# Attention and soft MoE on one core: one batch-end store, 2.5 groups by halves, smaller last slab pieces, and 32 weight rows on the hardware queue

## The chip, the core and the metric

The kernel runs on one core of one Trainium2 chip. The metric is the device time of one execution in microseconds (us). The kernel before took 181.37 us as the median of six runs (180.99 to 181.56).

The core has five instruction streams: PE (matmul; PEld is its weight load), DVE (vector), ACT (scalar), POOL and SP. The profile counts 16 DMA engines. Two DMA queues matter. The loads of q, k, v and of nearly all weights go from POOL to the software queue, which the profile calls q0, and are cast from f32 to bf16 on the way: in the kernel before the profile has 30.41 MB on q0 for 60.82 MB of f32 (the 61.93 MB read in all, less the 1.11 MB of loads on q1). All stores, the first half of one weight and phi go from SP to the hardware queue, q1. A transfer is cut into packets (18900 in all in the kernel before). A transfer of 128 partitions lands in 16 parts, whose times the trace gives. It does not name the DMA engine of a packet or of a part: where an engine is said to be ahead or late, one of the 16 parts was, and that a part is an engine's is my reading.

## The reference, cut to what matters

```python
# q, k, v: (8 batches, 8 heads, 576 tokens, 64)
scores = q @ k.transpose(0, 1, 3, 2) / 8
# heads 0-3: a causal window of 32; heads 4-7: 128 wide, each fourth key
attn = softmax(where(mask, scores, -1e9)) @ v
x = attn.transpose(0, 2, 1, 3).reshape(4608, 512)        # 4608 = 8 * 576

# soft MoE: 8 experts with 4 slots each; phi (512, 32), w1 (8, 512, 1024), w2 (8, 1024, 512)
logits = x @ phi
slot_input = softmax_over_tokens(logits).T @ x           # (32, 512)
slot_out[e] = relu(slot_input[e] @ w1[e]) @ w2[e]        # four rows for each expert
return softmax_over_slots(logits) @ slot_out             # (4608, 512), f32
```

Two facts shape the end. No output row can be finished before the last part of w2 is there, because each row mixes all slots. And 576 tokens are 4 × 128 + 64, so the last 64 tokens of each batch do not fill 128 partitions with four rows each; the kernel gathers the ends of all eight batches in a ninth group of 512 rows, called the batch-end group here.

## The kernel before

The loads are issued in a fixed order: q, k, v of all batches with w1 between them, then w2. The last expert's w2 comes in two column slabs of 256, each in pieces of 4, 2 and 2 of its eight row chunks.

```python
def w1_piece(e, hf, r0=0, n=2):                 # one half of an expert's w1, all 128 partitions
    def fn():
        return pool.dma_start(
            a(o_w1 + e * 4096 + hf * 2048 + 1024 * r0, [[1, 1024 * n]]),
            moe_w1[e, 256 * hf:256 * hf + 256, :].rearrange("(p two) f -> p (two f)", two=2)
            [:, 1024 * r0:1024 * (r0 + n)])
    return (fn, n << 19, f"w1_{e}{hf}", [b_w1[e]])
# ... cut ...
for s in range(2):
    wq += [w2_slab(6, s), w2_slab(7, s, 0, 4), w2_slab(7, s, 4, 2),
           w2_slab(7, s, 6, 2)]
```

L2 is the product with w2. A tile of output needs its columns of L2's sum. Phase 1 works on columns 0 to 255 and phase 2 on columns 256 to 511; for the first two groups (`NA`) the tiles are made by column halves, so that their first halves can be stored before the last slab has landed.

```python
for x in (1, 2):                                # the two column slabs of experts 6 and 7
    l2((6,), x, 256 * x - 256, 256, bufs=[b_w2[6][x - 1]])
    for y, cs in enumerate((range(4), range(4, 6), range(6, 8))):
        l2((7,), x, 256 * x - 256, 256, cs, [b_w2h[y][x - 1]])
    op(DVE, lambda x=x: dve.tensor_tensor(...))  # adds the earlier experts' sum: "the add"

NA = 2
# ... cut ...
def tok(G, j):                                  # 128 tokens: each fourth of a group of 512
    return (a(o_et + 576 * G + j, [[4, 128]]) if G < 8 else
            a(o_tail + j, [[4, 128]]))

def store(G, c0, cw, prio, j0=0, n=4):
    # ...
    for p0 in [0] if G < 8 else range(0, 128, 16):   # batch ends: eight stores of 16 partitions
        pn = 128 if G < 8 else 16
        dst = out[576 * G:576 * G + 512] if G < 8 else out[36 * p0 + 512:36 * p0 + 576]
        dst = dst[:, c0:c0 + cw].rearrange("(p j) f -> p j f", j=4)
        store_ops.append(op(SP, lambda p0=p0, pn=pn, dst=dst: spq.dma_start(
            dst[:, j0:j0 + n, :],
            af(ostg(G) + 2 * (512 * j0 + c0), [[512, n], [1, cw]], p0, pn)), ...))

halves = [(n // 2, n % 2 * 2) for n in range(int(2 * NA))]
# phase 1: tiles and stores of columns 0-255 of `halves`; phase 2: columns 256-511 of them,
# then whole rows of the other groups in order 2, 3, ..., 8 (the batch ends last)
```

The softmax here doesn't subtract the row's maximum and nothing guards it: scores larger than these inputs give would overflow.

## Time and profile before

| | before |
|---|---|
| time, median of six runs | 181.37 us |
| span of the profiled run, and its granted TensorE clock | 179.8 us, 0.945 |
| last part of w2 ("the last slab") landed | 152.60 us |
| first store that needs it landed | 156.91 us |
| the last full 1 MB store landed | 174.38 us |
| the last batch-end store landed | 179.31 us |

The granted clock is the share of its full speed that PE was allowed; it changes between 0.5 and 1.0 within a run (kernel before: 1.00 to 146.4 us, 0.50 to 153.2, 1.00 to 166.8, then 0.50). The kernel is bound by DMA. These are lines of the page of the kernel before: in the first two, each of the 40 columns is a fortieth of the span; then the queues with packets, MB and share of the time of 16 engines.

```profile
DMA  5999999999999999999999999999999999799995
GB/s 184 233 210 211 214 209 213 215 208 213 213 210 215 212 209 210 215 211 208 215 211 211 215 210 214 214 214 211 215 211 213 197 196 235 243 401 408 425 346 162
...
q0 software_dynamic: 15024, 30.41, 89.6%
q1 hardware_dynamic: 3856, 10.55, 16.5%
...
HBM read 61.93 MB, written 9.44 MB: 397 GB/s over the span
```

Slices 2 to 34 are all 9, full. Then comes a 7 (the change from loads to stores), then stores at 400 GB/s and over, and at the very end 346 and 162 GB/s. (A cast load is counted by its bf16 result, 30.41 MB on q0 for 60.82 MB read, so 213 GB/s there is about 426 GB/s of reading.) PE is busy 70% of the span and DVE 65%, so they wait for DMA. Time can only come from uneven engines, from gaps and from poor transfers. The windows show where these are; the columns are the start and end, the length, each engine's busy time with its instructions, the granted clock, the mean DMA share and the rate.

```profile
core 0: us, PE busy (x) PEld busy (x) DVE busy (x) ACT busy (x) POOL busy (x), PEclk, DMA share, GB/s
...
20.00:24.00 4.00, 3.40 (x77) 2.40 (x76) 3.97 (x8) 3.15 (x4) 1.97 (x4) 1.00 1.08 213
152.60:156.90 4.30, 3.75 (x21) 1.92 (x21) 3.10 (x7) 2.79 (x7) 0.00 (x0) 0.93 0.71 240
155.10:155.60 0.50, 0.50 (x4) 0.30 (x4) 0.50 (x2) 0.50 (x3) 0.00 (x0) 1.00 0.00 0
169.40:171.90 2.50, 0.00 (x0) 0.00 (x0) 0.00 (x0) 0.00 (x0) 0.00 (x0) 0.50 1.01 419
174.40:179.30 4.90, 0.00 (x0) 0.00 (x0) 0.00 (x0) 0.00 (x0) 0.00 (x0) 0.50 0.72 187
```

- **The end.** A 1 MB store of 128 partitions takes 2.50 us at 419 GB/s. The batch ends are 1 MB too, but take 4.9 us at 187 GB/s. No engine works then, so all of it is span. In the trace, 8 KB packets of these eight stores take up to 1.47 us where those of the other stores take 0.31.
- **The gap.** From 155.1 to 155.6 us nothing moves at all. The stores of the first halves have been sent, and those that need the last slab are not ready.
- **The run-up.** The trace gives for each transfer the times at which its 16 parts landed. Around 10 us a load's parts land within 0.5 us; the last slab's lie 2.72 us apart, and fall in two clumps: seven within 0.65 us of the first, one at 1.29, eight at 2.39 to 2.72. The latest part decides when L2 can go on: the last part of the first column slab landed at 147.24 us and the next matmul began at 147.28. Over the run, 16 instruction fetches of 16 KB go out, one each 7 us or so, and each takes 0.9 to 1.0 us. The landings of the kernel before follow them step by step. Before the first fetch (22.52 us) the latest part of a load on q0 is 0.50 to 0.65 us behind the first part; after it one part is 1.62 to 1.79 behind; with each fetch up to the eighth (72.91) there is one more, and then eight are 1.25 to 1.60 behind. After the ninth (80.22) one of them is over 2.6 behind, and after the sixteenth (137.25) eight are, by 2.37 to 2.77. So a fetch puts one part about 1 us back, and the lag of the last slab fits two fetches for each of eight parts. Which engines these are, the trace does not tell.

What the last slab releases is seen in the chain of waits of the kernel before (start, length, what ran) and then in the timeline of DVE (start, length, operation, in brackets the idle time before it and what ended that).

```profile
115.41 31.83 DMA ar<-in_moe_w_dram
147.28 0.62 PE ps L857 x2
147.93 0.44 DVE ar L881
...
150.37 2.89 PE ps L857 x16
153.29 0.44 DVE ar L881
153.77 0.42 PE ps L901 x2
154.22 8.90 DVE ar L913 x15
```

```profile
153.29 0.43 DVE L881 TENSOR_TENSOR ar<-ps,ar 64x256 bf16<-64x256 f32 x1 [2.40 <-PE ps L857]
154.22 4.95 DVE L913 TENSOR_SCALAR ar<-ps,fs 128x256 f32<-128x256 f32 x9 [0.51 <-PE ps L901]
```

The add (line 881) of the last slab starts at 153.29, 0.69 us after the landing at 152.60, behind L2's matmuls (line 857); the first output tiles follow at 154.22. The way from the landing to the first store that needs it (156.91) is 4.31 us.

### The profile page before, as it was taken

The numbers are of one execution on the slowest core, as the hardware profiler recorded it, in microseconds if no ns is written. First come the engines' busy times: TensorE is split into PE (matmuls) and PEld (weight loads), VectorE is DVE, ScalarE is ACT, GpSimd is POOL, SyncE is SP. The second block draws the span as 40 slices with busy tenths as digits, with TensorE's granted clock in tenths as the row PEclk, the third lists the DMA queues.
The fourth block names the chain that finished last, engine by engine and source line by source line (L and its number), as shares of the span: only waits on it lengthen the run. The fifth ranks groups of instructions, "written<-read, shape, count | busy, mean of one in ns | idle before, by whom it ended". The sixth has DMA issues, their size and how long they took to land.

```text
span 179.8 us, 4781 instructions
## 1 busy us (share of the span) xinstructions
PE 125.4 (70%) x2092; PEld 84.5 (47%) x2092; DVE 116.9 (65%) x219; ACT 104.9 (58%) x164; POOL 50.9 (28%) x101
## 2 busy tenths in 40 slices
PE   0008877987989899899789889885775469892000
PEld 0005645764767667666567667674431125420000
DVE  6898789779798798898699699291200104797000
ACT  2406598796798788787688788945020103794000
POOL 7559742242334134133930000951000000000000
PEclk9999999999999999999999999999999975999555
DMA  5999999999999999999999999999999999799995
GB/s 184 233 210 211 214 209 213 215 208 213 213 210 215 212 209 210 215 211 208 215 211 211 215 210 214 214 214 211 215 211 213 197 196 235 243 401 408 425 346 162
DMA packets 18900, 41.26 MB, mean 230 GB/s; under 512 B 1984, under 2 KB 8128, under 8 KB 17984
## 3 DMA queue, kind: packets, MB, share of 16 engines
q0 software_dynamic: 15024, 30.41, 89.6%
q1 hardware_dynamic: 3856, 10.55, 16.5%
q8 instruction: 16, 0.26, 0.5%
q14 instruction: 4, 0.03, 0.0%
HBM read 61.93 MB, written 9.44 MB: 397 GB/s over the span
## 4 chain that ended last, share of the span: by engine, by line
DMA 59%; DVE 20%; PE 6%; ACT 3%; issue 2%; POOL 2%; DVEq 0%
DMA ar<-in_k_dram 41%; DMA ar<-in_moe_w_dram 18%; DVE ar L488 6%; DVE ar L913 6%; DVE ar L614 2%; PE ps L857 2%; DVE ar L445 2%; PE ps L901 1%; POOL ar L371 1%; ACT ar L548 1%; DVE ar L450 1%; PE ps L509 1%; ACT ar L576 1%; ACT ar L670 1%; POOL ar L364 1%
## 5 line engine op out<-in xcount | busy, mean ns | idle before, releaser
L488 DVE STREAM_TRANSPOSE ar<-ar 128x576 uint32<-128x576 uint32 x40 | 48.5, 1239 | 7.7 <-DMA ar<-in_k_dram 7.7
L548 ACT ACTIVATE ar<-ps 128x1152 bf16<-128x1152 f32 (+1 forms) x32 | 38.0, 1186 | 20.6 <-PE ps L533 11.4
L509 PE MATMUL ps<-ar 128*128 128x320 bf16 (+1 forms) x128 | 22.7, 301 | 15.6 <-DVE ar L488 13.1
L614 DVE TENSOR_TENSOR ar<-ps,fs 96x768 bf16<-96x768 f32 (+1 forms) x32 | 26.3, 823 | 1.3
L576 ACT ACTIVATE ar<-ps 128x768 bf16<-128x768 bf16 x32 | 24.8, 810 | 2.2 <-PE ps L570 2.1
L509 PEld LDWEIGHTS ps<-ar 128*128 128x128 bf16 x128 | 10.5, 99 | 20.2 <-POOL ar L418 13.1
L570 PE MATMUL ps<-ar 128*128 128x128 bf16 x192 | 15.9, 229 | 3.8 <-DVE ar L614 3.4
L603 PE MATMUL ps<-ar 128*128 128x65 bf16 x320 | 14.7, 193 | 3.3 <-ACT ar L548 3.2
L910 ACT ACTIVATE ar<-ps,fs 128x512 f32<-128x512 f32 (+1 forms) x22 | 11.4, 656 | 8.7 <-PE ps L901 8.7
L857 PE MATMUL ps<-ar 128*32 128x512 bf16 (+1 forms) x80 | 11.7, 374 | 6.0 <-DMA ar<-in_moe_w_dram 5.4
L335 POOL DMA_DIRECT2D ar<-in_k_dram x16 | 8.9, 555 | 24.8 <-DVE ar L488 15.6
L570 PEld LDWEIGHTS ps<-ar 128*128 128x128 bf16 x192 | 12.4, 118 | 5.7 <-DVE ar L614 4.0
L603 PEld LDWEIGHTS ps<-ar 128*128 128x128 bf16 x320 | 12.0, 97 | 6.0 <-ACT ar L548 3.7
L913 DVE TENSOR_SCALAR ar<-ps,fs 128x512 f32<-128x512 f32 (+1 forms) x22 | 12.6, 649 | 1.3 <-PE ps L901 1.3
L364 POOL DMA_DIRECT2D ar<-in_moe_w_dram x12 | 6.4, 580 | 20.8 <-DVE ar L488 20.8
L335 POOL DMA_DIRECT2D ar<-in_q_dram x16 | 8.8, 547 | 10.5 <-DVE fs L610 5.0
L901 PE MATMUL ps<-ar 128*128 128x512 bf16 (+1 forms) x44 | 10.7, 372 | 1.4 <-DVE ar L881 1.1
L610 DVE RECIPROCAL fs<-ps 96x12 f32<-96x12 f32 (+1 forms) x32 | 6.2, 195 | 7.9 <-PE ps L603 7.6
L670 ACT ACTIVATE ar<-ps 128x576 bf16<-128x576 bf16 x16 | 9.6, 652 | 3.1 <-PE ps L654 3.1
L335 POOL DMA_DIRECT2D ar<-in_v_dram x16 | 8.8, 549 | 8.8 <-DVE fs L610 5.5
L857 PEld LDWEIGHTS ps<-ar 128*32 128x32 bf16 x80 | 5.0, 104 | 12.3 <-DMA ar<-in_moe_w_dram 8.8
L693 PE MATMUL ps<-ar 128*128 128x288 bf16 x64 | 9.2, 287 | 1.2 <-ACT ar L677 1.2
(75 smaller groups left out, 186.7 us busy)
## 6 DMA issues: line engine op xcount, KB each, us to landing
ar<-in_moe_w_dram POOLq DMA_DIRECT2D x29, 512.0 KB, 27.5
out_dram<-ar SPq DMA_DIRECT2D x5, 1024.0 KB, 8.1
ar<-in_k_dram POOLq DMA_DIRECT2D x16, 288.0 KB, 23.4
ar<-in_q_dram POOLq DMA_DIRECT2D x16, 288.0 KB, 23.5
ar<-in_v_dram POOLq DMA_DIRECT2D x16, 288.0 KB, 23.6
out_dram<-ar SPq DMA_DIRECT2D x8, 256.0 KB, 3.4
ar<-in_moe_w_dram SPq DMA_DIRECT2D x1, 1024.0 KB, 5.0
out_dram<-ar SPq DMA_DIRECT2D x2, 512.0 KB, 4.0
```

Source lines behind the costliest of these rows:

```text
L335: return pool.dma_start(a(o_stg + (s * 3 + j) * 1152, [[1, 1152]]), src[b, 4 * dl:4 * dl + 4].rearrange("h (p t) d -> (h p) (t d)", p=32))
L488: return dve.transpose(au(o_dst, [[1, 18], [18, 32]]), au(src, [[32, 18], [1, 32]]))
L509: pe.matmul(pf(h, 0, [[1, W]]), a(o_id, [[1, 128]]), a(msk, [[1, W]]), start=True, stop=False)
L548: eo = op(ACT, lambda P=P, W=W: act.activation(a(P, [[W, 4], [1, W]]), AP(ps, 0, [[4096, 128], [512, 4], [1, W]]), ACTF.Exp, scale=SCALE), ...
L570: last = pe.transpose(pb(bank.idx, bb * 256 + par * 32, [[64, 4], [1, 32]]), src, a(o_id, [[1, 128]]))
L576: op(ACT, lambda t=t, bank=bank: act.activation(a(o_vb[vs] + 3 * t * VBK, [[66, 12], [2, 32], [1, 2]]), pb(bank.idx, 0, [[64, 12], [1, 32] ...
L603: last = pe.matmul(pf(bank.idx + x, 65 * t, [[1, 65]]), w, a(VB + t * VBK + 66 * h, [[1, 65]]), start=True, stop=True)
L614: op(DVE, lambda hp=hp, bank=bank: dve.tensor_tensor(a(ox + 128 * hp, [[64, 2], [256, NT], [1, 64]], 0, rows), pf(bank.idx, 0, [[512, 2], ...
L857: last = pe.matmul(pf(sobank[x].idx, 0, [[1, n]], 32 * j, 32), a(o_htz + 1024 * g + 128 * c + 32 * j, [[1, 32]]), a(w2off(e) + DM * c + co ...
L901: op(PE, lambda: pe.matmul(pf(bank.idx, 0, [[1, cw]]), tok(G, j), a(o_so + c0, [[1, cw]]), start=True, stop=True), pet(1, cw), prio, reads ...
L910: op(ACT, lambda: act.activation(dst, src(), ACTF.Copy, scale=sca), actt(cw, .1), prio + .1, reads=[bank, b_rinv], writes=wr, name=f"OE{G} ...
L913: op(DVE, lambda: dve.tensor_scalar(dst, src(), sca, None, op0=AluOp.mult), dvet(cw, True) + .08, prio + .1, reads=[bank, b_rinv], writes= ...
```

## The change

Its intent: less work after the last slab, a fuller gap, a faster end, and less on the load queue. It has four parts.

1. **One store for the batch ends.** The copy that gathers them puts them in the order (token quad, batch) and the store covers all 128 partitions; its destination has an outer dimension of 16, then 8. It is also moved from the last place to the middle, after group 2.
2. **2.5 groups by halves** for 2: one more 256 KB store (a phase-1 store) ahead of the last slab.
3. **Last slab pieces of 4, 2, 1, 1** for 4, 2, 2.
4. **32 partitions of one w1 piece** (96 to 127 of expert 0's second half) go over the hardware queue as f32, in transfers of five adjacent partitions, to a buffer that is still free; POOL casts them later.

```diff
-    def w1_piece(e, hf, r0=0, n=2):
+    def w1_piece(e, hf):
+        pn = 96 if (e, hf) == (0, 1) else 128
# ... the rest of the piece: [:pn] of the source, partitions 0..pn ...
-               w2_slab(7, s, 6, 2)]
+               w2_slab(7, s, 6, 1), w2_slab(7, s, 7, 1)]
# ... cut ...
+    def load_w1g(after):
+        src = moe_w1[0, 256:512, :].rearrange("(p two) f -> p (two f)", two=2)
+        for p0, pn in [(96 + 5 * n, 5) for n in range(6)] + [(126, 2)]:
+            op(SP, lambda p0=p0, pn=pn: spq.dma_start(
+                af(w2off(3), [[1, 2048]], p0, pn), src[p0:p0 + pn]), ..., writes=b_w2[3], ...)
+        op(POOL, lambda: pool.tensor_copy(
+            a(o_w1 + 2048, [[1, 2048]], 96, 32), af(w2off(3), [[1, 2048]], 96, 32)), ...)
# ... cut: load_w1g(first_t[3]) is called in batch 1 ...
-        a(o_tail, [[64, 8], [1, 64]]), a(o_et + 512, [[576, 8], [1, 64]])), ...
+        a(o_tail, [[4, 8], [32, 16], [1, 4]]), a(o_et + 512, [[576, 8], [4, 16], [1, 4]])), ...
-        for y, cs in enumerate((range(4), range(4, 6), range(6, 8))):
+        for y, cs in enumerate((range(4), range(4, 6), range(6, 7), range(7, 8))):
-    NA = 2
+    NA = 2.5
-        for p0 in [0] if G < 8 else range(0, 128, 16):
# ... cut: the store before, shown above ...
+        if G < 8:
+            dst = out[576 * G:576 * G + 512, c0:c0 + cw].rearrange("(p j) f -> p j f", j=4)[:, j0:j0 + n, :]
+            src = af(ostg(G) + 2 * (512 * j0 + c0), [[512, n], [1, cw]])
+        else:
+            dst = out.rearrange("(b r) f -> b r f", b=8)[:, 512:576, :].rearrange("b (i j) f -> i b (j f)", j=4)
+            src = af(ostg(G), [[1, 2048]])
+        store_ops.append(op(SP, lambda: spq.dma_start(dst, src), ...))
-    for n in range(int(2 * NA), 18):
-        G, x = n // 2, n % 2 * 2
+    for G, x in [(2, 2)] + [(G, x) for G in (8, 3, 4, 5, 6, 7) for x in (0, 2)]:
```

More of the change, by code (lines that the diff above doesn't have):

```diff
@@ L309, in bass_dilated_sliding_attn__then__soft_moe_slots_kernel @@
     b_w5h = [Buf(f"w5h{x}") for x in range(2)]
-    b_w2h = [[Buf(f"w2h{x}{s}") for s in range(2)] for x in range(3)]
+    b_w2h = [[Buf(f"w2h{x}{s}") for s in range(2)] for x in range(4)]
     b_htz, b_tail, b_so = Buf("htz"), Buf("tail"), [Buf("soA"), Buf("soB")]
@@ L351, in w_sem @@
         return shared[key]
-    def w1_piece(e, hf, r0=0, n=2):
+    def w1_piece(e, hf):
+        pn = 96 if (e, hf) == (0, 1) else 128
         def fn():
             return pool.dma_start(
-                a(o_w1 + e * 4096 + hf * 2048 + 1024 * r0, [[1, 1024 * n]]),
-                moe_w1[e, 256 * hf:256 * hf + 256, :].rearrange("(p two) f -> p (two f)", two=2)
-                [:, 1024 * r0:1024 * (r0 + n)])
-        return (fn, n << 19, f"w1_{e}{hf}", [b_w1[e]])
+                a(o_w1 + e * 4096 + hf * 2048, [[1, 2048]], 0, pn),
+                moe_w1[e, 256 * hf:256 * hf + 256, :].rearrange("(p two) f -> p (two f)", two=2)[:pn])
+        return (fn, pn << 13, f"w1_{e}{hf}", [b_w1[e]])
     def w2_piece(e, c0):
@@ L373, in fn @@
                 moe_w2[e].rearrange("(p c) f -> p c f", c=8)[:, c0:c0 + n, 256 * s:256 * s + 256])
-        return (fn, n << 17, f"w2s_{e}{s}{c0}", [b_w2[e][s] if n == 8 else b_w2h[(0, 4, 6).index(c0)][s]])
+        return (fn, n << 17, f"w2s_{e}{s}{c0}", [b_w2[e][s] if n == 8 else b_w2h[(0, 4, 6, 7).index(c0)][s]])
     for e in range(8):
@@ L406, in bass_dilated_sliding_attn__then__soft_moe_slots_kernel @@
             1.1, -200.0, reads=b_w2[4], writes=[b_w1[0]], name=f"w1c{x}")
+    s_w1g = sem("s_w1g")
+    def load_w1g(after):
+        src = moe_w1[0, 256:512, :].rearrange("(p two) f -> p (two f)", two=2)
+        for p0, pn in [(96 + 5 * n, 5) for n in range(6)] + [(126, 2)]:
+            op(SP, lambda p0=p0, pn=pn: spq.dma_start(
+                af(w2off(3), [[1, 2048]], p0, pn), src[p0:p0 + pn]), .1, -50.0, kind="dma",
+               nbytes=pn << 13, lag=4.0, sem=s_w1g, after=[after], writes=b_w2[3], name=f"w1g{p0}")
+        op(POOL, lambda: pool.tensor_copy(
+            a(o_w1 + 2048, [[1, 2048]], 96, 32), af(w2off(3), [[1, 2048]], 96, 32)), 2.5, 0.0,
+           reads=b_w2[3], writes=[b_w1[0]], name="w1gc")
     def const_ops():
@@ L762, in bass_dilated_sliding_attn__then__soft_moe_slots_kernel @@
             load_phi(first_t[0])
+        if i == 1:
+            load_w1g(first_t[3])
     names = [w[2] for w in wq]
@@ L795, in bass_dilated_sliding_attn__then__soft_moe_slots_kernel @@
     op(POOL, lambda: pool.tensor_copy(
-        a(o_tail, [[64, 8], [1, 64]]), a(o_et + 512, [[576, 8], [1, 64]])), .8, T1 + 4, reads=[b_et],
+        a(o_tail, [[4, 8], [32, 16], [1, 4]]), a(o_et + 512, [[576, 8], [4, 16], [1, 4]])), .8, T1 + 4, reads=[b_et],
        writes=[b_tail], name="tail")
@@ L919, in store @@
               if c0 < 256 * (s + 1) and c0 + cw > 256 * s]
-        for p0 in [0] if G < 8 else range(0, 128, 16):
-            pn = 128 if G < 8 else 16
-            dst = out[576 * G:576 * G + 512] if G < 8 else out[36 * p0 + 512:36 * p0 + 576]
-            dst = dst[:, c0:c0 + cw].rearrange("(p j) f -> p j f", j=4)
-            store_ops.append(op(SP, lambda p0=p0, pn=pn, dst=dst: spq.dma_start(
-                dst[:, j0:j0 + n, :],
-                af(ostg(G) + 2 * (512 * j0 + c0), [[512, n], [1, cw]], p0, pn)), .1, prio, kind="dma",
-                nbytes=pn * n * cw * 4, rate=347e3 if cw < 512 else 420e3,
-                sem=sem(f"s_o{G}{c0}{j0}{p0}"), reads=rd, name=f"ST{G}{c0}{j0}{p0}"))
+        if G < 8:
[4 more added lines that the diff above has]
+            src = af(ostg(G), [[1, 2048]])
+        store_ops.append(op(SP, lambda: spq.dma_start(dst, src), .1, prio, kind="dma",
+                            nbytes=128 * n * cw * 4, rate=347e3 if cw < 512 else 420e3,
+                            sem=sem(f"s_o{G}{c0}{j0}"), reads=rd, name=f"ST{G}{c0}{j0}"))
     T2 = T1 + 40
@@ L939, in bass_dilated_sliding_attn__then__soft_moe_slots_kernel @@
         store(G, 256, 256, T2 + 10 + G + .25 * x + .2, x, 2)
-    for n in range(int(2 * NA), 18):
-        G, x = n // 2, n % 2 * 2
+    for G, x in [(2, 2)] + [(G, x) for G in (8, 3, 4, 5, 6, 7) for x in (0, 2)]:
+        at = G if G < 8 else 2.6
         for j in (x, x + 1):
-            out_tile(G, j, 0, 512, T2 + 10 + G + .25 * x)
-        if G == NA:
-            store(G, 0, 512, T2 + 10 + G + .25 * x + .2, x, 2)
+            out_tile(G, j, 0, 512, T2 + 10 + at + .1 * x)
+        if G < NA:
+            store(G, 0, 512, T2 + 10 + at + .1 * x + .1, x, 2)
         elif x:
-            store(G, 0, 512, T2 + 10 + G + .5)
+            store(G, 0, 512, T2 + 10 + at + .3)
     order = sc.run([4, 5, 6, 7], [0, 1, 2, 3], last_ex[0])
```

## The prediction

> **What bounds it now.** DMA. In the page's row of DMA slices every slice from 2 to 34 reads 9; 61.93 MB read and 9.44 MB written make 397 GB/s over the 179.8 us span. PE (70%) and DVE (65%) wait. Time can only come from unevenness, gaps and poor transfers.
>
> Read from the landings of each transfer's 16 parts:
> - The load queue's engines drift apart. A load's first and last part land 0.5 us apart at 10 us, 2.72 us apart at 152.6 us (last slab): then eight engines are 2.4 to 2.7 us behind the first, seven less than 0.7. The sixteen 16 KB instruction fetches, one each 7 us, fit that: about 1.1 us on one engine each.
> - After the last slab (152.60) come L2 matmuls, add and first tiles; the first full store lands at 156.91. First-half stores fill only to 155.39; from 155.1 to 155.6 the DMA share is 0.
> - The eight 128 KB batch-end stores take 174.38 to 179.31, 4.93 us for 1 MB; 1 MB stores of 128 partitions land each 2.50 us. Their 8 KB packets take up to 1.47 us instead of 0.31. [...]
>
> **What the change does.**
> 1. One batch-end store for eight: up to -2.43 us, all on the path. Doubt: the destination's outer dimension is now 16[...], and it could still cost 4.9 us. 65% for the good case.
> 2. 2.5 groups by halves: one more 256 KB store (0.67 to 0.77 us) in the gap, -0.5 us; but two more tiles (0.43 us on ACT and DVE) ahead of the second half's L2, where PE at half clock has 0.1 us of slack: gives back 0.2 to 0.3.
> 3. Pieces 4/2/1/1: one matmul less after the last landing, -0.2 us. POOL's extra issues run 30 us ahead.
> 4. 32 w1 partitions on the hardware queue: 2 rows (0.31 us each) less on all engines, 6 or 7 extra on five. [...] If those are among the engines ahead, the last slab lands 0.6 us earlier; if not, up to 1.3 us later. [...] 70% for the gain. The POOL copy (0.60 us for 512 columns; 2.4 for 2048) is off the path: issues are 23 us ahead of landings.
>
> Attention has slack: L2 waits for w2 from 135.6 us.
>
> **Sum.** All good: -2.4 -0.6 -0.4 = -3.4, 178.0 us. Weighted with the doubts: **178.6 us**, range 177.3 to 180.6. Faster by over 2%: 0.22; within 2%: 0.75; slower by over 2%: 0.03.
>
> **What would show it.** (1) The batch-end store lands 2.5, not 4 to 5, us after the one before; about 419 GB/s to the end. (2) DMA share near 155 us no longer 0; five half stores. (3) One matmul between the last slab's landing and the add. (4) The last slab's parts land within about 2.1 us, the last near 152.0.
>
> **What would make it wrong.** [...]the wrong five engines; PE becoming the limit before the second half; engines that stay uneven through the stores.

Its sum: −2.4 (point 1: 4.93 − 2.50 us), −0.6 (point 4: two rows of 0.31 us less on each engine) and −0.4 (points 2 and 3, net) make −3.4, so 178.0 us from 181.4, and 178.6 with the doubts. That one store could still cost 4.9 us, and that five engines get 6 or 7 rows each, stand as estimates. So do the 2.4 us for the POOL copy, four times its 0.60; it took 1.89 in the kernel after.

## The result, and the profile after

Ratios here are the mean time of one kernel's fast runs over the mean of the other's fast runs of the same rounds, so they are not quite the ratio of the medians that are quoted. Where the text gives a kernel's distance from before in us, it is (ratio − 1) × 181.4.

| | before | after |
|---|---|---|
| time, median of six runs (range) | 181.37 (180.99 to 181.56) | 182.74 (182.17 to 183.23) |
| ratio, 95% interval | | 1.0077 (1.0053 to 1.0102), +1.4 us |
| span of the profiled run, clock | 179.8, 0.945 | 181.2, 0.943 |
| parts of the v load near 30 us: first, last | 27.16, 28.81 | 27.77, 31.79 |
| last slab landed (parts apart) | 152.60 (2.72) | 154.82 (4.26) |
| first store that needs it landed | 156.91 | 158.97 |
| the batch-end store, from the landing before it | 4.93 (eight, last) | 5.04 (one, in the middle) |
| last store landed (parts apart) | 179.31 (1.03) | 180.78 (1.54) |

The kernel after is 0.8% slower. That is inside the "within 2%" class, but outside the predicted range of 177.3 to 180.6.

The last stores of the two profiled runs differ by 1.47 us, and the landings split it. The last slab is 2.22 us later; from it to the first store that needs it the kernel after takes 4.15 us instead of 4.31, so 0.16 less; from there to the end 21.81 instead of 22.40, so 0.59 less. 2.22 − 0.16 − 0.59 = 1.47. All of the loss is there before the last slab lands, and most of it by 32 us.

The page of the kernel after, the same lines as before:

```profile
DMA  5999999999999999999999999999999999899996
GB/s 190 232 208 195 205 180 214 212 210 213 213 211 214 211 210 213 213 210 213 212 210 211 216 208 215 213 215 212 213 214 214 197 195 211 291 363 255 416 427 262
...
q0 software_dynamic: 15024, 30.28, 89.3%
q1 hardware_dynamic: 4208, 10.81, 17.0%
...
HBM read 61.93 MB, written 9.44 MB: 394 GB/s over the span
```

The DMA row looks the same: the row says how long packets are under way, not what they move. The GB/s row shows it. Slices 4 to 6 (about 13.6 to 27 us) read 195, 205, 180 where before has 211, 214, 209. These are the slices in which the w1 rows go over the hardware queue. And the slow stretch of the end, 346 and 162 in the two last slices before, is now the 255 in slice 37, with 262 in the last. The windows of the kernel after:

```profile
core 0: us, PE busy (x) PEld busy (x) DVE busy (x) ACT busy (x) POOL busy (x), PEclk, DMA share, GB/s
...
20.00:24.00 4.00, 3.62 (x78) 2.42 (x76) 3.96 (x7) 2.93 (x4) 1.97 (x4) 1.00 1.18 179
154.80:159.00 4.20, 3.42 (x19) 2.04 (x21) 3.31 (x8) 3.00 (x8) 0.00 (x0) 1.00 0.83 287
157.00:157.50 0.50, 0.35 (x2) 0.30 (x4) 0.50 (x2) 0.50 (x3) 0.00 (x0) 1.00 0.22 76
163.50:168.50 5.00, 1.02 (x3) 0.25 (x3) 3.23 (x5) 1.95 (x4) 0.00 (x0) 0.89 0.97 279
168.50:171.00 2.50, 0.00 (x0) 0.00 (x0) 0.00 (x0) 0.00 (x0) 0.00 (x0) 0.50 1.00 419
178.30:180.80 2.50, 0.00 (x0) 0.00 (x0) 0.00 (x0) 0.00 (x0) 0.00 (x0) 0.50 0.49 206
```

- From 20 to 24 us the DMA share **rose** from 1.08 to 1.18 while the rate **fell** from 213 to 179 GB/s. More packet time is spent on fewer bytes. In the trace the 8 KB packets of the 32 rows take 0.31 to 0.99 us, half of them over 0.71; such a packet by itself takes 0.32.
- The gap near 157 us is partly filled: 76 GB/s and a share of 0.22 where the corresponding stretch before had 0. The whole stretch of 4.2 to 4.3 us after the slab has a share of 0.83 for 0.71.
- From 163.5 to 168.5 us, in which the batch-end store lands and the next one begins, the queue moves 279 GB/s with a share of 0.97. That is again a busy queue that moves little; the stores around it have 419. It no longer stands at the end, but it costs the same, and the last window shows the end ragged.

And the chain of waits and DVE's timeline after, to be read against those of before:

```profile
121.58 33.23 DMA ar<-in_moe_w_dram
154.86 0.30 PE ps L874
155.18 0.44 DVE ar L898
155.67 0.42 PE ps L918 x2
156.12 8.64 DVE ar L930 x15
```

```profile
155.18 0.43 DVE L898 TENSOR_TENSOR ar<-ps,ar 64x256 bf16<-64x256 f32 x1 [2.16 <-PE ps L874]
156.12 5.35 DVE L930 TENSOR_SCALAR ar<-ps,fs 128x256 f32<-128x256 f32 x10 [0.51 <-PE ps L918]
```

One matmul (line 874) of 0.30 us now stands between the landing (154.82) and the add (155.18): 0.36 us for 0.69. Only a third of this is the pieces' doing. The clock granted just after the landing was 0.50 in the kernel before and 1.00 here; d_one_store and e_flat (below), with the old pieces and a clock of 1.00, need 0.47 us, and c_w1g_only, with the old pieces and 0.50, needs 0.63. So the smaller piece is worth 0.11 us and the clock of that run 0.22. The 4.15 us for 4.31 to the first store have the same flaw: d_one_store, with the old pieces, has 4.15 too.

### The profile page after: what moved, and what is told of

It reads as the page before. It is cut to its first block, busy times and chain, and to the rows that moved or that the text cites. A ratio compares the mean times of both kernels' runs of the same rounds, so it can differ in the third digit from the quotient of the medians.

```text
span 181.2 us, 4788 instructions
## 1 busy us (share of the span) xinstructions
PE 126.8 (70%) x2093; PEld 84.9 (47%) x2094; DVE 117.6 (65%) x220; ACT 105.1 (58%) x165; POOL 53.6 (30%) x104
## 4 chain that ended last, share of the span: by engine, by line
DMA 60%; DVE 19%; PE 4%; POOL 4%; issue 2%; ACT 1%; DVEq 0%
DMA ar<-in_k_dram 42%; DMA ar<-in_moe_w_dram 18%; DVE ar L503 6%; DVE ar L930 5%; POOL ar L372 3%; DVE ar L629 2%; DVE ar L460 2%; PE ps L524 2%; DVE ar L465 1%; PE ps L585 1%; PE ps L531 1%; ACT ar L685 1%; ACT ar L563 1%; POOL ar L365 1%; DVE ar L509 1%
## 5 line engine op out<-in xcount | busy, mean ns | idle before, releaser
L503 DVE STREAM_TRANSPOSE ar<-ar 128x576 uint32<-128x576 uint32 x40 | 49.2, 1244 | 10.6 <-DMA ar<-in_k_dram 9.8
L918 PE MATMUL ps<-ar 128*128 128x512 bf16 (+1 forms) x45 | 9.7, 339 | 1.5 <-DVE ar L898 1.0
```

The source lines that it names most:

```text
L503: return dve.transpose(au(o_dst, [[1, 18], [18, 32]]), au(src, [[32, 18], [1, 32]]))
```

## The experiments

All kernels below gave a correct result. Landings are those of each kernel's profiled run. The kernels ran in five groups, and those of one group ran on the same chip beside the kernel before, whose median was 181.54, 181.44, 181.41, 181.30 and 181.36 us in the first to the fifth. Each kernel had 4 to 6 timed runs.

**The theory**: in the transfers of five adjacent partitions the rows slow one another down (the text calls it the loss by adjacent rows), and this costs about 2 us before the last slab. **The rival**: the loss comes from the end (the moved, single store, or the extra tiles), or from the mere presence of the rows on the hardware queue, adjacent or not. That the rows burden five engines fits the kernel after: the semaphore of its seven transfers has 32 updates from 20.29 to 27.37 us, one for each row (and seven before, 0.42 to 0.47 us after each issue), where a transfer of 128 partitions has 16; and of the v load near 30 us five parts are 3.29 to 4.02 us behind the first, one 2.03 and the other ten at most 0.89. Why rows that are adjacent should be slow, no trace shows. One reading is left untested by all that follows: rows that are adjacent in SBUF are also adjacent 8 KB pieces of w1 in memory, and every edit of the step between them moves both. That adjacency costs time is tested; where the cost arises is not.

### c_w1g_only: the kernel before with part 4 alone

```diff
+        pn = 96 if (e, hf) == (0, 1) else 128          # in w1_piece, as in the change
+    def load_w1g(after): ...                           # seven SP transfers and the POOL cast, as in the change
```

> The kernel before plus the hardware-queue part of w1 alone. Theory: this part is the whole loss. The five engines it loads stay about 3.3 to 4 us behind from 30 us on, the last slab (before: landed 152.60 us, parts 2.72 us apart) lands near 154.8 with its parts about 4.2 us apart, and the time is 183.3 to 183.9 us (before 181.4). Rival: the loss comes from the changes at the end of the kernel; then this one is at 180.8 to 181.4 us with a last slab at or before 152.6.

Measured (first group): 183.58 us (182.89 to 183.86), ratio 1.0108 (1.0083 to 1.0134), +2.0 us. The last slab landed at 154.67, its parts 4.94 us apart, and the last store at 181.41. So part 4 alone gives more than the whole loss, with the old end in place; time and landing are those of the theory. Its window from 20 to 24 us, however, shows less than that of the kernel after, whose share was 1.18 with 179 GB/s:

```profile
20.00:24.00 4.00, 4.00 (x65) 2.87 (x63) 3.93 (x8) 1.59 (x2) 1.52 (x4) 1.00 1.10 209
```

### a_no_hwq: the kernel after without part 4

```diff
-        pn = 96 if (e, hf) == (0, 1) else 128
+        pn = 128
-        if i == 1:
-            load_w1g(first_t[3])
```

> The changed kernel with its hardware-queue part of w1 taken out again (the whole w1 piece on the software queue). Theory: the last slab lands at 152.4 to 152.7 us again, 2.2 us earlier, and the time is 180.2 to 180.8 us (changed kernel 182.7): what is left of the change is worth at most 1 us, most of it from the one store. Rival (the transfers of five hurt only because of what comes after them, or the unevenness is made up for by the stores): it stays above 181.5 us.

Measured (second group): 180.90 us (180.64 to 180.99), ratio 0.9966 (0.9952 to 0.9981), −0.6 us; the last slab at 152.52, where the kernel before has it. Taken with the kernel after, part 4 costs 2.0 us here too. The time is 0.1 us over the expected band. The batch-end store in the middle took 5.05 us (161.08 to 166.13), so the rest of the change together gains only 0.6.

### b_spread: the same five partitions a transfer, but six partitions apart

```diff
-        for p0, pn in [(96 + 5 * n, 5) for n in range(6)] + [(126, 2)]:
+        for p0, pn, st in [(96 + n, 5, 6) for n in range(6)] + [(126, 2, 1)]:   # st: partition step
```

The rows of a transfer, the bytes, the packets and the place in the program are the same.

> The changed kernel, with the same seven transfers, the same bytes, rows per engine and issue times, but each transfer of five takes partitions six apart (96, 102, ..., 120) instead of five adjacent ones. Theory [...] the five engines lose only about 1.2 to 1.5 us, the last slab lands at 152.0 to 152.4 (changed kernel 154.82) and the time is 179.9 to 180.5 us (changed kernel 182.7). Rival (extra rows on the hardware queue cost 0.55 us each on these engines whatever their partition[...], or the engines are the wrong ones): nothing changes, 182.4 to 183.0 us and a last slab near 154.8.

Measured (first group): 181.21 us (180.88 to 181.73), ratio 0.9986 (0.9962 to 1.001), −0.25 us. The expected band was missed by 0.7 us, but 1.65 of the 2.0 us are back. The packets of the rows now take 0.31 to 0.32 us, all of them (those of the last transfer too, whose two rows are still adjacent). The windows from 20 to 24 us, first of b_spread and then of a_no_hwq:

```profile
20.00:24.00 4.00, 3.48 (x77) 2.41 (x76) 3.97 (x8) 3.07 (x4) 1.98 (x4) 1.00 1.08 237
```

```profile
20.00:24.00 4.00, 4.00 (x64) 2.99 (x62) 3.93 (x8) 1.63 (x2) 1.59 (x4) 1.00 1.08 214
```

The share is 1.08 in both. (The 237 GB/s hold f32 rows, which count double against cast ones, so this is no better use.) With adjacent rows it was 1.18 and 179 in the kernel after, and 1.10 and 209 in c_w1g_only.

The excess of packet time tells how far the loss by adjacent rows reaches. For 14.5 to 29 us, I summed over all packets what each took above what such packets take otherwise (0.19 us for 2304 bytes, 0.32 for 4 KB and for a row). The load queue's sum is split at 18.5 us, just before the first row's packet (18.58 to 19.28 us). p_adj5 (adjacent rows) and n_own5 (rows apart) are a pair further below:

```
              load queue      load queue      8 KB rows   4-byte packets     (us of packet time)
              before 18.5     from 18.5                   of the rows' queue
before            0.0             0.3             -            0.1
after             6.2            15.8           10.7           3.7
c_w1g_only        4.0             2.1            7.4           1.8
p_adj5            1.6             2.0            6.7           4.2
b_spread          3.1             1.3            0.0           0.4
n_own5            1.7             0.7            0.0           0.4
```

What the three kernels with adjacent rows share is the loss of the rows themselves, 6.7 to 10.7 us; spread over five engines that is an estimate of 1.3 to 2.1 us for each. The load queue's own packets lose more than the rows in the kernel after alone, 15.8 us. In c_w1g_only, which is slower by as much, they lose 2.1, so this is not what makes the 2 us. The last slab's landings agree. Its latest part is 2.30 us later in the kernel after than in a_no_hwq, 2.07 in c_w1g_only than in the kernel before, and 1.34 in p_adj5 than in n_own5; the mean of its 16 parts is 1.82, 0.82 and 0.53 us later. The latest part decides, and in c_w1g_only and p_adj5 a few late engines are enough for it. What made the 15.8 us is not shown; the other two kernels have 2.1 and 2.0. What the load queue loses before 18.5 us, while phi's small packets are in flight, is not from the rows' packets, which have not begun; kernels without rows lose 0.0 to 1.8 us there.

Why b_spread missed: one 2304-byte packet at 15.74 us took 1.55 us instead of 0.19, while phi's 256-byte packets were in flight, and one part of the last slab was alone at its end (153.24; the next one 152.52). That both are of one engine is my reading. Kernels without rows have such packets there too, but shorter (0.79 us in a_no_hwq, 0.85 in f_ends). Whether that is chance or belongs to the edit, one profile does not tell.

### d_one_store: the kernel before with one batch-end store, in the last place

```diff
-        a(o_tail, [[64, 8], [1, 64]]), a(o_et + 512, [[576, 8], [1, 64]])), ...
+        a(o_tail, [[4, 8], [32, 16], [1, 4]]), a(o_et + 512, [[576, 8], [4, 16], [1, 4]])), ...
# and the one store, as in the change; order and everything else as before
```

> The kernel before with its eight batch-end stores of 16 partitions replaced by the one store, still last. Theory [...]: the last store still lands 4.9 to 5.1 us after the one before it, and the time is the same as before, 181.2 to 181.8 us. Rival (in the changed kernel its 5.04 us came from its place among the other stores or from the uneven engines): it lands about 2.5 us after the one before, 178.8 to 179.2 us.

Measured (first group): 180.56 us (180.53 to 180.65), ratio 0.9948 (0.9933 to 0.9963), −0.9 us. The store took 4.02 us (174.29 to 178.31): the middle between the theory's 4.9 to 5.1 and the rival's 2.5, so neither was right. Its windows, a full store and then the batch ends:

```profile
169.00:171.50 2.50, 0.00 (x0) 0.00 (x0) 0.00 (x0) 0.00 (x0) 0.00 (x0) 0.50 1.01 419
174.30:178.30 4.00, 0.00 (x0) 0.00 (x0) 0.00 (x0) 0.00 (x0) 0.00 (x0) 0.50 0.75 201
```

In the trace most of the first half of this store's packets take 0.5 to 0.9 us, and over half of the later ones 0.31 to 0.34. Of 16 packets in a row from 174.46 us, 15 take 0.60 to 0.67, twice 0.31. The eight stores before had 16 partitions each; their slow packets mostly take 0.8 to 1.5 us, and they took 4.93. Why the packets of either form are slow, and less so with the one store, is not shown: the trace does not name a packet's engine.

### l_store_last: a_no_hwq with the one store put last again

```diff
-    for G, x in [(2, 2)] + [(G, x) for G in (8, 3, 4, 5, 6, 7) for x in (0, 2)]:
-        at = G if G < 8 else 2.6
+    for G, x in [(2, 2)] + [(G, x) for G in (3, 4, 5, 6, 7, 8) for x in (0, 2)]:
+        at = G
```

> The changed kernel without its hardware-queue part (180.90 us), and with the one batch-end store moved from the middle back to the end. Theory: in the middle the store costs 5.05 us on the slowest engine and leaves the parts of all later stores 1.4 us apart to the end; as the last store it cost 4.02 us. So it lands 3.9 to 4.2 us after the one before it and the time is 179.7 to 180.2 us. Rival (its place makes no difference): 180.7 to 181.1 us.

Measured (third group): 180.04 us (179.97 to 180.13), ratio 0.9925 (0.9912 to 0.9938), −1.4 us; the batch-end store took 4.03 us (173.69 to 177.72), as in d_one_store. So the move to the middle costs about 0.75 us by the ratios. In the middle this store ends ragged: in a_no_hwq its parts land 1.60 us apart, and those of each later store 1.41 to 1.42, to the end, where the stores before it had 0.34. The following stores do not even them out. They do even out where the queue runs dry: from 2.65 us at the last slab of that kernel to 0.31 at the first store that needed it, and in the kernel before, where the DMA share was 0.00 from 155.1 to 155.6 us, from 2.72 to 0.23.

### e_flat: the kernel before with nine groups of 512 consecutive rows

If the store's cost comes from its odd form, then a store that is never odd should take 2.5 us. In the flat output, 4608 rows are nine groups of 512; no group needs to stop at a batch's end.

```diff
     def tok(G, j):
-        return (a(o_et + 576 * G + j, [[4, 128]]) if G < 8 else
-                a(o_tail + j, [[4, 128]]))
+        return a(o_et + 512 * G + j, [[4, 128]])
# the row sums of each group, formerly a column of the transposes of its batch:
+            for j in range(4):
+                last = pe.matmul(pf(bank.idx, 363 + j, [[1, 1]]), tok(b, j), a(o_rm, [[1, 1]]), ...)
# the copy of the batch ends goes; every store:
+        dst = out[512 * G:512 * G + 512, c0:c0 + cw].rearrange("(p j) f -> p j f", j=4)[:, j0:j0 + n, :]
```

> The kernel before with the nine output groups cut as 512 consecutive rows of the whole output, so that every store, the last too, has 128 partitions at one even step on both sides (the row sums for the scale are taken for these groups, by four more one-column matmuls for each batch; no batch-end gather). Theory: the last store then costs 2.5 us like the others instead of 4.93, so 178.7 to 179.3 us. Rival (the last 1 MB is slow because of where it lies in memory or because it is last): 181 us or more.

Measured (first group): 178.98 us (178.89 to 179.25), ratio 0.9862 (0.9843 to 0.9882), −2.5 us. The last store takes 2.48 us (174.33 to 176.81), and its windows, a store in the row and then the last, show it moving 315 GB/s where d_one_store had 201:

```profile
171.80:174.30 2.50, 0.00 (x0) 0.00 (x0) 0.00 (x0) 0.00 (x0) 0.00 (x0) 0.50 1.01 419
174.30:176.80 2.50, 0.00 (x0) 0.00 (x0) 0.00 (x0) 0.00 (x0) 0.00 (x0) 0.50 0.76 315
```

This is the 2.4 us that the prediction hoped for from the one store. It was on the path, but the one store was not the way to it. It also answers the doubt whether the time of a last store is some fixed cost: it is not.

### f_ends and g_pieces: parts 2 and 3, and part 3 alone

```diff
# both: pieces of 4/2/1/1
-               w2_slab(7, s, 6, 2)]
+               w2_slab(7, s, 6, 1), w2_slab(7, s, 7, 1)]
-        for y, cs in enumerate((range(4), range(4, 6), range(6, 8))):
+        for y, cs in enumerate((range(4), range(4, 6), range(6, 7), range(7, 8))):
# f_ends only
-    NA = 2
+    NA = 2.5
```

> The kernel before with 2.5 groups by halves and 4/2/1/1 slab pieces alone (eight batch-end stores, still last; no hardware-queue part). Theory: a fifth 256 KB store fills the gap after the last slab, worth its 0.67 to 0.77 us less what PE loses before the second half; the time from the last slab's landing to the first full store's landing goes from 4.31 to 4.1 to 4.4 us and the total falls by 0.3 to 0.6 us, to 180.8 to 181.2. Rival (PE at half clock is the limit there, so that the two added tiles cost as much as the store gains): 181.3 us or more.

> The kernel before with 4/2/1/1 slab pieces alone. Theory: one matmul of about 0.2 us less between the last slab's landing and the add: 181.2 to 181.3 us, with the first full store landing 0.1 to 0.2 us sooner after the last slab. Rival (all of the 0.5 us that this and the halves gave together comes from the pieces): 180.9 to 181.0 us.

Measured: f_ends (second group) 180.94 us (180.78 to 181.07), ratio 0.9971 (0.9959 to 0.9984), −0.5 us; g_pieces (third group) 181.43 us (181.11 to 181.68), ratio 0.9996 (0.9983 to 1.0009), nothing. The band of 181.2 to 181.3 for g_pieces was missed by 0.1 us. So the half-us is that of the halves, unless the pieces help only together with them. The gap of before in f_ends:

```profile
155.10:155.60 0.50, 0.50 (x4) 0.23 (x2) 0.50 (x3) 0.50 (x2) 0.00 (x0) 1.00 0.62 217
```

From a share of 0.00 to 0.62. The two tiles more ahead of the last slab cost about 0.14 us by two profiles: the first store that needs the slab came 4.18 us after it, in g_pieces, which differs only in the halves and had the same clock of 1.00 there, 4.04. (The 4.31 of the kernel before, at half clock, is no measure for this.)

### h_flat_ends: e_flat with parts 2 and 3

```diff
+    # e_flat, and in it the lines of f_ends
```

> The same two parts on top of the kernel with even stores of 512 consecutive rows. If they add up: 0.3 to 0.6 us under that kernel's 178.98, so 178.4 to 178.7 us. If they are worth nothing: 178.9 to 179.1 us.

Measured (second group): 178.36 us (178.14 to 178.41), ratio 0.9825 (0.9812 to 0.9839), −3.2 us; the last slab at 152.76, the last store at 176.13. The gains add up: −2.5 and −0.5.

### j_flat_ends_w8, k_own32 and m_own64: the rows in transfers of eight, four partitions apart

Can part 4 gain anything once its rows are not adjacent? Here they go in transfers of eight partitions, four apart. The three kernels are h_flat_ends with the rows of partitions 96 to 127, 0 to 31 and 0 to 63.

```diff
+        for p0 in range(96, 100):                                    # j_flat_ends_w8
+        for p0 in [32 * h + r for h in range(1) for r in range(4)]:  # k_own32; range(2) in m_own64
+            op(SP, lambda p0=p0: spq.dma_start(
+                AP(ar_f.tensor, (p0 * NBF + w2off(3)) // 2, [[4 * NBF // 2, 8], [1, 2048]]),
+                src[p0:p0 + 29:4]), ...)
```

> The former plus the 32 partitions of w1 on the hardware queue, in four transfers of eight partitions four apart[...]. Theory (the idea of the change was right[...]): 8 KB packets of 0.32 us, the last slab 0.5 to 0.7 us earlier than in the former, with its parts at most 2.3 us apart, and 177.8 to 178.2 us. Rival (the engines that get the rows are not those that are ahead, or rows on the second queue cost more than they save): the last slab no earlier than 152.6 and 178.5 us or more.

> The even-store kernel with both end parts, and 32 partitions of the w1 piece on the hardware queue in four transfers of eight, four apart, but now partitions 0 to 31 and not 96 to 127. Theory: in the run with 96 to 127 the eight engines that are behind lost what they had been relieved of[...]; with 0 to 31[...] the engines that are behind gain their 0.6 us in full, the last slab lands at 152.0 to 152.3 us (152.76 without this part, 153.10 with 96 to 127), and the time is 177.6 to 178.0 us. Rival (rows on the second queue cost the engines more than they save, wherever they go): as with 96 to 127, 178.4 us or more.

> The same with 64 partitions, 0 to 63, in eight transfers. Theory: the engines that are behind gain 1.2 us and come out ahead;[...] the last slab lands with parts at most 1.9 us apart and between 151.7 and 152.4 us; 177.4 to 178.1 us. Rival: twice the cost of the former run's rows, 179 us or more.

Measured, j in the second group, k and m in the third: 178.60 us (178.49 to 178.73), ratio 0.9842 (0.9828 to 0.9856); 178.59 us (178.51 to 178.62), ratio 0.9844 (0.9831 to 0.9857); and 179.33 us (179.2 to 180.6), ratio 0.9898 (0.9876 to 0.9919). Against h_flat_ends with 0.9825 none gains, and 64 rows lose over a us. All three theories missed, and all three times lie where the rivals had put them. The landings of k_own32, expected at 177.6 to 178.0, suggest what happens. At 28.22 us a load's parts fall into two clean halves, eight engines at 0 to 0.20 and eight at 1.05 to 1.45 us: as if the rows sat on eight engines, each with four rows (about 1.3 us), and all 16 were relieved of two rows (0.6 us). At the last slab, 3.44 us apart, two parts are by themselves at the late end (3.19 and 3.44) and two at the early one (0 and 0.21). That fits eight engines with rows of which two are among the eight that are late anyway, and two engines with neither. Eight is then the wrong number. It is a count that fits; the trace does not name the engines.

### n_own5 and p_adj5: partitions 0 to 31 by fives, apart or adjacent

```diff
+        for p0, pn, st in [(n, 5, 6) for n in range(6)] + [(30, 2, 1)]:       # n_own5
+        for p0, pn, st in [(5 * n, 5, 1) for n in range(6)] + [(30, 2, 1)]:   # p_adj5
```

These are h_flat_ends with the rows of partitions 0 to 31; they differ from one another in the step alone.

> The even-store kernel with both end parts (178.36 us), plus 32 partitions of w1 on the hardware queue: partitions 0 to 31, in transfers of five, six apart. In the two runs with transfers of eight the relieved engines did gain 0.6 us by 28 us, but at the end two of the eight loaded engines were last, 0.8 to 1.0 us behind the rest[...]. Theory: five is the right number[...], the parts of the last slab land at most 2.4 us apart, it lands at 152.0 to 152.4 us (152.76 without the rows) and the time is 177.7 to 178.1 us. Rival (rows moved to the second queue never pay): 178.4 us or more.

> The same bytes, engines and partitions 0 to 31, but each transfer of five takes adjacent partitions, as in the changed kernel. Theory (adjacency itself is the fault[...]): 8 KB packets of 0.6 us and more, the five engines are last at the end by over 1 us, the last slab lands after 153.6 us and the time is 179.2 to 180.4 us. Rival[...]: as with six apart, within 0.3 us.

Measured (fourth group): n_own5 178.34 us (178.21 to 178.91), ratio 0.9835 (0.9822 to 0.9849); p_adj5 179.48 us (178.95 to 179.91), ratio 0.9897 (0.9877 to 0.9918). n_own5's theory missed: the parts lie 3.37 us apart and not 2.4, the slab lands no earlier than without rows, and the time is that of h_flat_ends. p_adj5's held in time and landing, though its packets were expected at 0.6 us and more. Adjacency alone costs 1.1 us here: the rows' packets take 0.32 to 0.87 us in p_adj5, 0.52 at the median, and 0.31 to 0.32 in n_own5; the last slab lands at 154.13 (parts 4.39 us apart) instead of 152.79 (3.37). The windows, first of p_adj5 and then of n_own5:

```profile
20.00:24.00 4.00, 3.33 (x76) 2.32 (x76) 3.97 (x8) 3.23 (x4) 1.97 (x4) 1.00 1.10 211
```

```profile
20.00:24.00 4.00, 4.00 (x64) 2.89 (x62) 3.93 (x8) 1.63 (x2) 1.58 (x4) 1.00 1.05 229
```

This is the cleanest of the pairs, since nothing but the step changed and both ran in one group. The cost is less than the 1.65 us between after and b_spread; why is not known.

In n_own5's profile the last product of attention came only at 134.42 us, PE's granted clock was 0.5 from 128.1 to 141.7 us, and PE ran behind: the add of the first slab came at 149.64 us, 2.5 us after its weights had landed (147.12), where the kernel before needs 0.7. That was a doubt about all kernels with flat groups, and led to the next pair.

### q_h11 and r_n11: the same with the instruction order of before

In e_flat, four tiny matmuls were added to each batch and the planned length of that step had been raised with them; the scheduler then ordered the instructions differently. Here the planned length is put back; nothing of the work is changed. r_n11 is q_h11 with the rows of n_own5.

```diff
-        op(PE, et_fn, pet(15, 33), pr("ET"), ...)
+        op(PE, et_fn, pet(11, 33), pr("ET"), ...)
```

> The even-store kernel with both end parts, in the order of instructions of the kernel before (the planned length of the row-sum matmuls, which the order is computed from, put back; nothing else changes). In the even-store runs so far the last attention product came 5 us later (131.8 us against 126.6 before), L1 ran in a stretch of half clock, and L2's first part ended only after its weights had landed, so the load queue's end did not decide alone. Theory: the last product is back near 127 us, L2 waits for its weights again, and the time is 177.9 to 178.4 us. Rival (the delay is from the added matmuls themselves): unchanged, 131 us or later.

> The same order with the 32 partitions of w1 (0 to 31, in fives, six apart) on the hardware queue. Theory: with PE waiting for the slabs again, their landing decides, which these rows bring forward by 0.3 to 0.6 us: 0.2 to 0.6 us faster than the former. Rival (rows moved to the second queue do not pay[...]): within 0.15 us of the former or slower.

Measured (fifth group): q_h11 178.26 us (178.13 to 178.47), ratio 0.9827 (0.9814 to 0.9841); r_n11 178.37 us (178.07 to 178.82), ratio 0.9837 (0.9822 to 0.9853). The order was changed as meant, as DVE's timelines show for the last product of attention, first in h_flat_ends and then in q_h11:

```profile
131.79 0.68 DVE L749 TENSOR_TENSOR ar<-fs,ps 32x512 bf16<-32x512 f32 x1 [1.25 <-PE ps L741]
```

```profile
128.25 0.67 DVE L749 TENSOR_TENSOR ar<-fs,ps 32x512 bf16<-32x512 f32 x1 [2.47 <-PE ps L741]
```

It comes 3.5 us earlier, and the time does not change (0.9825 to 0.9827): attention has that slack. q_h11 fell in its band; r_n11's theory missed and its rival held. With the rows, six apart, r_n11's last slab lands 0.23 us earlier (152.60 for 152.83), and the time is no different. The rows seem to be on engines that were ahead: in q_h11 seven parts of the last slab land within 0.58 us, one at 1.23 and eight at 2.27 to 2.94, in r_n11 three within 0.39 and thirteen at 2.02 to 2.87, as if five of the early ones had joined the late. But the engines' mean end at the last slab is 0.37 us **later** than in q_h11: about 6 us of engine time more. The load queue's packets of 14.5 to 29 us took 4.3 us above the usual in r_n11 and 2.0 in q_h11, which is about 2 of the 6. The rest is left open.

q_h11 and h_flat_ends are the best versions (n_own5 and r_n11 lie within the intervals), 1.7% faster than before and 2.5% faster than after by their ratios.

## Why the prediction was wrong

The time was predicted at 178.6 us with 177.3 to 180.6, and measured at 182.74. The parts, by the experiments:

| part | predicted | measured | from |
|---|---|---|---|
| 1, one store, in last place | up to −2.43, good case 65% | −0.9 | d_one_store |
| 1, its move to the middle | not costed | +0.75 | a_no_hwq, l_store_last |
| 2, halves | −0.5, gives back 0.2 to 0.3 | −0.5 | f_ends, g_pieces |
| 3, pieces | −0.2 | 0.0 | g_pieces |
| 4, rows on the hardware queue | −0.6 at 70%, else up to +1.3 | +2.0 | after, a_no_hwq, c_w1g_only |
| sum | | +1.35 | after: +1.4 |

The move and part 4 come from the kernel after itself and the kernels next to it, so that the sum closes is a check of the first ones only, and a weak one.

**The step that failed** is point 4: "If those are among the engines ahead, the last slab lands 0.6 us earlier; if not, up to 1.3 us later." The last slab landed 2.2 us later. The bound of 1.3 us is four rows or so of 0.31 us on the wrong engines; it treats a row as a packet that costs its usual time. A sentence after it doubted that adjacent partitions go at full speed together, but no number was put to it, and it did not enter the bound. The runs show what that term was: a row took 0.71 us at the median in the kernel after (0.61 in c_w1g_only, 0.52 in p_adj5) instead of 0.32, 6.7 to 10.7 us more in all, or an estimate of 1.3 to 2.1 us on each of five engines. So it seems that engines that had been ahead became the last: within 1.29 us of its first part the last slab has eight parts in the kernel before and three in the kernel after. Its latest part came 1.34 to 2.30 us later for it. Changing only the step between the partitions returns 1.65 us (b_spread) or 1.1 us (p_adj5 to n_own5). The load queue's packets lost 15.8 us more while the rows were under way in the kernel after, but only 2.1 in c_w1g_only with the same loss of time. What could have been known in advance is the size: the trace of before already had 8 KB packets of up to 1.47 us, in the stores of 16 adjacent partitions.

**The range left out the prediction's own doubts.** With the doubt of point 1 and the worse case of point 4, its own terms give 181.4 − 0 (point 1) − 0.2 (point 2) − 0.2 (point 3) + 1.3 (point 4) = 182.3 us, past the upper end of 180.6. And both points carried the same doubt, that adjacent partitions are slow together, so that it was likely to come true in both or in neither.

**The gain in it was too large as well.** "70% for the gain" of 0.6 us: six apart, with packets of 0.31 to 0.32 us in n_own5, the rows brought 0.23 us of slab time at most (r_n11) and none of run time. The arithmetic "2 rows less on all engines, 6 or 7 extra on five" fits as a count (five late parts near 30 us in the kernel after; the landings of k_own32 fit the same arithmetic for eight engines, with 0.6 us of relief), but bytes were moved and not removed, so the sum over engines had nothing to gain and only balance could pay; and the mean end of the engines came 0.37 us later, which took that back. Why it did is for the most part open.

**Point 1 was rightly doubted and wrongly weighted.** That the one store "could still cost 4.9 us" came true in kind, and the 65% for the good case was not earned: nothing in the trace of before spoke for it. With the move, point 1 brought 0.2 us of its 2.43, a shortfall as large as the loss by point 4. The size is 4.02 us in last place, less than feared; its packets are slow in the first half (0.5 to 0.9 us) and mostly normal later (0.31 to 0.34); in the middle, where the raggedness of its parts then stays to the end, the store took 5.04 and nearly nothing of the gain was left. That the move has a cost was not seen at all.

**Point 2 was right**, and better than its net of −0.2 to −0.3: the gap's share went from 0 to 0.62, and the feared cost of 0.2 to 0.3 us was about 0.14 (f_ends against g_pieces, one profile each).

**Point 3 was right in its mechanism**, one matmul less, but this is worth 0.11 us from landing to add at a clock of 1.00 (0.36 for 0.47) and nothing in time. In g_pieces the first store that needs the slab comes 4.04 us after it, 0.11 less than in d_one_store with the old pieces at the same clock, and the slab lands 0.18 us later than in the kernel before (152.78 for 152.60), which takes it back; both differences are of one profile each.

**What bounds the kernel** was read rightly: DMA throughout, the two weak places in the windows were real, and both could be had (e_flat −2.5, f_ends −0.5). The change simply repaired the larger one in a way that kept most of its cost, and paid 2 us for a third.

## What to carry to other kernels

Before building on a transfer of a new shape, time it beside one known to be even; a transfer that covers all 128 partitions is not even by that alone (1 MB took 2.48 us as an even store in e_flat, and 4.02 us in d_one_store as one store with a destination whose outer size is 16). Look for the loss in the durations of single packets and in the landings of a transfer's parts: rows of 0.52 to 0.71 us instead of 0.32 and a last slab 4.3 to 4.9 us apart were there in all three kernels with adjacent rows, while the share that rose as the rate fell (1.18 and 179 GB/s) was clear in one of them only. Read a wait for matmuls together with the granted clock of that moment: it made two thirds of what looked like the gain of the smaller pieces. Where a shape is awkward (576 = 4 × 128 + 64), look first whether the output can be cut so that the awkward shape does not arise: that took 2.5 us where the better awkward store took 0.9.
